# Who issues a kernel's small transfers: two of eight hash-row copies moved from GpSimd to ScalarE, and four of the last turned piece's stores moved from SyncE to GpSimd

## The chip, the cores and the metric

The kernel runs on one core of one Trainium2 chip. The metric is the device time of one execution in microseconds, the median of several runs. Engines are named as the profile names them: PE is TensorE (PEld its weight loads), DVE is VectorE, ACT is ScalarE, POOL is GpSimd, SP is SyncE. SyncE, ScalarE and GpSimd issue the DMA transfers; a "q" behind an engine's name (SPq, ACTq) stands for its sequencer, which does the issuing.

## What is computed

Hash-bucketed attention with 4 batches, 8 heads, 768 positions and a head dimension of 64, followed by a two-layer block with a per-channel PReLU. All arrays are float32 in value (the weights arrive in wider words, which the kernel turns into float32 itself). Cut to what matters:

```python
q_bits = (einsum('bhsd,dk->bhsk', q, proj) > 0)      # 6 hash bits for each row of q and k
k_bits = (einsum('bhsd,dk->bhsk', k, proj) > 0)
mask = q_bucket[:, :, :, None] == k_bucket[:, :, None, :]
scores = where(mask, q @ k.T / sqrt(D), -1e9)
attn = softmax(scores) @ v                           # (B, H, S, D)
x = attn.transpose(0, 2, 1, 3).reshape(3072, 512)
h = x @ w_in                                         # 512 -> 2048
g = maximum(h, 0) + alpha * minimum(h, 0)
out = g @ w_out                                      # 2048 -> 512
```

## The kernel before

**Two stages.** The attention stage works through 16 pairs of heads (`pi`), one after the other. The second stage does the two products of the block for four batches, each product by a seven-product scheme (`ff1`, `ff2`, line 912 issues all their matmuls). Engine instructions are wrapped in `do(...)`, which keeps them in the order in which the program writes them. The DMA issues of the hash rows are not wrapped: a scheduler puts them in their place on the issuing engine.

**One attention pair.** `scores` (L773) makes 12 cells of scores for 128 keys by 384 queries of two heads. Each cell adds two products in one PSUM bank pair: a product of hash bits (`qb`, `kb`, bf16), which is large and negative where the buckets differ, and the product of the scaled `qT` and `kT` (float32). ScalarE turns each cell into exponentials (L784, into `pts`). Cells, turned inputs, hash sums and `totals` share three bank pairs (`two_banks`, L686). `attend` (L806) multiplies with v, and VectorE adds up the exponentials (L792 to L803) so that `totals` (L820) can sum them on TensorE. `divide` (L831) turns the sums on VectorE (L841), takes reciprocals and stores the result (L860).

**The hash rows.** While pair `pi` is in work, `hash_bits(pi + 1)` (L726, called at L1214) makes the next pair's bits. Eight small matmuls (L732) put the hash sums of both halves of q and k in one PSUM bank, and ScalarE's Sign pass (L736) writes them as the bf16 tile `hr`. The bits then have to go to other partitions: eight transfers of 12 rows and 9 KB each (L742), all issued by GpSimd, in the order k, k, q, q of the first half of the columns, then the same of the second half. They write `kb` (one buffer) and `qb` (two). Next on ScalarE is the scaling of the next pair's `qT` (L1215), then the rounding of the next weight piece (`weight_abs`, L599 and L603), the squares of q and k (L714) and another weight piece. On TensorE `attend` and `totals` follow the hash matmuls, and then the next pair's score cells, the first of which reads the first half's bits and the second, third and so on both halves' q bits.

**Weights on the side.** In each pair two raw weight pieces of 512 KB are loaded by GpSimd (`load_weight`, L585; one before the hash rows, one after them), rounded by ScalarE and VectorE, and stored for the second stage by SyncE (L654 and L667, the latter four stores of 448 KB as w_in_s). SyncE also loads q, k and v for later pairs. Early in the second stage GpSimd loads and stores eight pieces of w_out each (L999, L1006).

**Completion semaphores.** In the built program the transfers that GpSimd issues take eight semaphores in turn, and those that SyncE and ScalarE issue take eight others in turn, the two engines together. Each transfer but the first of a semaphore waits, on its issuing engine, for the landing of the transfer that used that semaphore before.

**The end.** Each batch's output pieces are turned in one of two ways. `turn_out` (L1071) turns a finished piece with VectorE (L1076) and stores it with 12 transfers of 32 KB (L1083). In the last block `turn_last` (L1088) turns pieces 5 and 4 of the last batch with TensorE, and ScalarE issues their three stores (L1105, L1114, L1116). `turn_out` runs at the end of each block but the last; for the last batch the pieces that reach it are 2 and 3, piece 3 in the last but one block. The test at L1082 names piece 5 of the last batch, which never comes through `turn_out`, so before the change SyncE issues all the stores there. After its last work each engine reads a flag, branches over a fallback version of the kernel (`general_path`), and waits for what is still open.

Of the kernel before, what the change touches and what calls it, by code (L numbers as in the profile page):

```python
# [407 lines left out]
def fast_path(  # L408
# [12 lines left out]
    nc = tc.nc  # L421
    P = 128
    B, H, S, D = q.shape
# [262 lines left out]
    def two_banks(name):  # L686
        return psum.tile([P, 2, 512], F32, name=name, tag="sc", bufs=3)
# [38 lines left out]
    def hash_bits(pi):  # L726

        ps = two_banks(f"hs{pi}")[:, 0, :CW]
        for half in range(2):
            for n, name in enumerate("kq"):  # L730
                c = D * n + 32 * half
                do(PE.matmul(  # L732
                    ps[c : c + 32], wh2, tr[name, pi][:, half * CW : (half + 1) * CW], start=True, stop=True,
                ))
        raw = pool.tile([P, CW], BF16, name=f"hr{pi}", tag="hr", bufs=1)
        do(ACT.activation(raw, ps, AF.Sign, bias=hb2))  # L736
        bits["q", pi], bits["k", pi] = qbs[pi % 2], kb
        for half in range(2):
            for n, name in enumerate("kq"):
                for s in range(2):  # L740
                    c = D * n + 32 * half + NB * s
                    nc.gpsimd.dma_start(  # L742
                        bits[name, pi][D * s : D * s + 2 * NB, half * CW : (half + 1) * CW], raw[c : c + 2 * NB],
                    )

# [325 lines left out]
    def turn_out():  # L1071
        while to_turn:
            b, p, half, ch = to_turn.pop(0)
            o = late[0].tile([P, CW, 2], F32, name=f"o{b}_{p}", tag="o")
            for i in range(2):
                do(DVE.transpose(o[:, :, i], m2[b, p][:, i]))  # L1076

            src = o.rearrange("p (c w d) i -> p c w (d i)", c=CH, d=32)
            for a in range(DM // 128):
                for c in range(CH):  # L1080
                    cols = slice(half * DM // 2 + 64 * a, half * DM // 2 + 64 * a + 64)
                    queue = nc.gpsimd if (b, p) == (B - 1, 5) and c % 2 else nc.sync  # L1082
                    queue.dma_start(  # L1083
                        out_v[b, ch * CH + c].rearrange("(w r) d -> r w d", r=32)[:, :, cols],
                        src[32 * a : 32 * a + 32, c],
                    )
# [90 lines left out]
    for pi in range(NPAIR):  # L1177
# [35 lines left out]
        if pi + 1 < NPAIR:  # L1213
            hash_bits(pi + 1)  # L1214
            do(ACT.activation(tr["q", pi + 1], tr["q", pi + 1], AF.Copy, scale=DOWN))  # L1215
# [38 lines left out]
    for j, (b, what, n) in enumerate(blocks):  # L1254
# [45 lines left out]
        if j + 1 < len(blocks):  # L1300
            turn_out()
        else:
            turn_last(0)
# [37 lines left out]
```

## Time and profile before

| | us |
|---|---|
| median of 3 runs (lowest, highest) | 880.37 (876.08, 881.94) |
| the profiled execution's own time | 880.52 |
| its span, first to last instruction | 878.6 |
| TensorE busy | 861.8 |
| VectorE busy | 749.9 |
| ScalarE busy | 361.4 |
| GpSimd busy | 130.4 |

The attention stage ends near 316 us, the second stage fills the rest. Times in the views are microseconds from the start of the span unless marked ns. A row of a timeline gives start, length, engine, line, operation, the tile it writes and the tile it reads, and in brackets how long the engine had been idle before it and what ended that. A row of a windows table gives the stretch, its length, then busy time and number of instructions of TensorE, its weight loads, VectorE, ScalarE and GpSimd, and at the end the granted TensorE clock, the busy share of the 16 DMA engines and their GB/s. An entry of the waits view gives total time, number of waits and the longest.

### The profile page before, as it was taken

How to read it: one execution, taken by the hardware profiler on the slowest of the kernel's cores; microseconds unless marked ns; L12 is line 12 of the kernel's file. 1: busy time of each engine (PE TensorE's matmuls, PEld its weight loads, DVE VectorE, ACT ScalarE, POOL GpSimd, SP SyncE). 2: the span in 40 equal slices, each digit the busy share in tenths (PEclk: the TensorE clock that was granted, in tenths of full speed). 3: DMA queues.
4: the chain of work that ended last, by engine and by line, in shares of the span. 5: the costliest groups of instructions: out<-in, count | busy, mean ns of one | idle time of the engine just before them, and what ended most of it. 6: DMA issues, size and time to landing. Idle time of an engine off the chain costs nothing.

```text
span 878.6 us, 14811 instructions
## 1 busy us (share of the span) xinstructions
PE 861.8 (98%) x5458; PEld 577.3 (66%) x5458; DVE 749.9 (85%) x1215; ACT 361.4 (41%) x654; POOL 130.4 (15%) x279
## 2 busy tenths in 40 slices
PE   9999999999998999999999999999999999999996
PEld 4444445444444445559996558996557997557996
DVE  6999989989997987999888769898668988668986
ACT  7776878878676752221112222112222112222111
POOL 1332544424433501120000000000000000000000
PEclk9999999999999999999999999999999999999998
DMA  8865886798696347685433426334435333520242
GB/s 195 174 150 125 196 215 151 166 215 219 166 257 154 116 146 264 209 302 219 147 122 94 167 90 198 112 124 115 141 121 155 142 118 99 176 84 1 96 153 68
DMA packets 171777, 135.36 MB, mean 154 GB/s; under 512 B 126976, under 2 KB 155824, under 8 KB 168112
## 3 DMA queue, kind: packets, MB, share of 16 engines
q1 hardware_dynamic: 158960, 108.44, 43.4%
q0 software_dynamic: 10320, 24.71, 9.3%
q10 hardware_dynamic: 2416, 1.18, 0.5%
q8 instruction: 45, 0.74, 0.3%
q14 instruction: 36, 0.29, 0.1%
HBM read 104.87 MB, written 28.31 MB: 152 GB/s over the span
## 4 chain that ended last, share of the span: by engine, by line
PE 61%; DVE 4%; issue 1%; POOL 0%; ACT 0%; DVEq 0%; ACTq 0%
PE f_0a L912 2%; PE z_4a L912 2%; PE z_7a L912 2%; PE z_3a L912 2%; PE z_6a L912 2%; PE z_5a L912 2%; PE f_4a L912 2%; PE f_3a L912 2%; PE f_2a L912 2%; PE f_1a L912 2%; PE z_2a L912 2%; PE f_5a L912 2%; PE z_1a L912 2%; PE f_7a L912 2%; PE f_6a L912 2%; PE z_2c L912 1%
## 5 line engine op out<-in xcount | busy, mean ns | idle before, releaser
L781 PE MATMUL sc<-qT,kT 64*128 64x384 f32 x768 | 157.4, 487 | 0.0
L784 ACT ACTIVATE pt<-sc 128x768 f32<-128x768 f32 x192 | 152.8, 812 | 8.2 <-PE sc L781 7.9
L814 PE MATMUL av<-pt,vn 128*32 128x385 f32 (+1 forms) x1536 | 127.0, 485 | 0.0
L814 PEld LDWEIGHTS av<-pt,vn 128*32 128x32 f32 x1536 | 50.3, 109 | 73.8 <-issue 71.7
L781 PEld LDWEIGHTS sc<-qT,kT 64*128 64x128 f32 x768 | 70.6, 189 | 41.4 <-issue 40.5
L781 PE MATMUL sc<-qb,kb 64*128 64x384 bf16 x384 | 66.7, 325 | 6.9 <-DMA qb<-hr 5.6
L965 DVE TENSOR_TENSOR g<-g,g 128x384 f32<-128x384 f32 x128 | 68.4, 555 | 2.2
L1029 DVE TENSOR_TENSOR gs<-g,gs 128x768 f32<-128x768 f32 x56 | 53.4, 953 | 1.0
L1029 DVE TENSOR_TENSOR gs<-g 128x768 f32<-128x768 f32 x56 | 53.3, 953 | 0.0
L1021 DVE TENSOR_TENSOR ws<-wl 128x512 f32<-128x512 f32 x56 | 38.5, 688 | 17.3 <-DMA wl<-w_out_s 16.3
L599 ACT ACTIVATE wr<-raw 128x512 int32<-128x512 uint32 x32 | 22.1, 692 | 64.2 <-issue 41.5
L781 PEld LDWEIGHTS <-kb 64*128 64x128 bf16 x384 | 22.0, 94 | 35.5 <-issue 12.3
L792 DVE TENSOR_TENSOR accp<-pt,pt 128x1536 f32<-128x1536 f32 x16 | 28.2, 1760 | 16.6 <-ACT pt L784 16.6
L961 DVE SCALAR_TENSOR_TENSOR g<-h,alpha 128x384 f32<-128x384 f32 x32 | 19.7, 617 | 24.9 <-ACT h L954 24.8
L742 POOL DMA_DIRECT2D kb<-hr x60 | 30.3, 507 | 24.1 <-ACT hr L736 23.5
L742 POOL DMA_DIRECT2D qb<-hr x60 | 29.8, 500 | 8.0 <-issue 4.3
L797 DVE TENSOR_TENSOR accd<-accd,pt 128x1536 f32<-128x1536 f32 x16 | 28.1, 1759 | 2.1 <-ACT kn L714 0.5
L803 DVE TENSOR_TENSOR accd<-accd,accp 128x1536 f32<-128x1536 f32 x16 | 28.1, 1758 | 0.6
L800 DVE TENSOR_TENSOR accp<-accp,pt 128x1536 f32<-128x1536 f32 x16 | 28.1, 1753 | 0.0
L796 DVE TENSOR_TENSOR accd<-pt,pt 128x1536 f32<-128x1536 f32 x16 | 28.0, 1752 | 0.0
L912 PE MATMUL f_0a<-x,wi 128*128 128x384 f32 x64 | 23.5, 489 | 0.0
L912 PE MATMUL f_4a<-x,wi 128*128 128x384 f32 x64 | 23.3, 486 | 0.0
(365 smaller groups left out, 1760.2 us busy)
## 6 DMA issues: line engine op xcount, KB each, us to landing
wi<-w_in_s SPq DMA_DIRECT2D x32, 896.0 KB, 4.7
wl<-w_out_s SPq DMA_DIRECT2D x16, 1024.0 KB, 4.8
wl<-w_out_r SPq DMA_DIRECT2D x12, 1024.0 KB, 4.9
raw<-in_moe_w_in_dram POOLq DMA_DIRECT2D x15, 512.0 KB, 5.2
raw<-in_moe_w_out_dram POOLq DMA_DIRECT2D x14, 512.0 KB, 4.8
w_in_s<-wsi SPq DMA_DIRECT2D x16, 448.0 KB, 6.6
qn<-in_q_dram SPq DMA_DIRECT2D x64, 96.0 KB, 5.2
vn<-in_v_dram SPq DMA_DIRECT2D x16, 384.0 KB, 5.9
```

Of the source, the lines that this page charges most:

```text
L742: nc.gpsimd.dma_start(bits[name, pi][D * s : D * s + 2 * NB, half * CW : (half + 1) * CW], raw[c : c + 2 * NB],)
L781: do(PE.matmul(sc[:, s, :CW], what["k", pi][r, ks], what["q", pi][r, qs], start=first, stop=not first,))
L784: do(ACT.activation(pts[kc][:, g, :, :CW], sc[:, :, :CW], AF.Exp, scale=SCALE / DOWN))
L792: do(DVE.tensor_tensor(accp[pi], p(0), p(1), op=ALU.add))
L797: do(DVE.tensor_tensor(accd[pi], accd[pi], p(5), op=ALU.add))
L800: do(DVE.tensor_tensor(accp[pi], accp[pi], p(2), op=ALU.add))
L803: do(DVE.tensor_tensor(accd[pi], accd[pi], accp[pi], op=ALU.add))
L814: do(PE.matmul(av[pi][D * s + t : D * s + t + 32, g, :w], nat["v", pi][:, s, kc * D + t : kc * D + t + 32], pts[kc][:, g, s, :w], start=(k ...
L912: do(PE.matmul(self.ps[bank], self.left(left, k), self.right(right, k), start=start and k == 0, stop=k == self.nk - 1, skip_group_check=no ...
L965: do(DVE.tensor_tensor(new_g(b, to)[:, i], g_m[b, x][:, i], g_m[b, y][:, i], op=ALU.subtract))
L1021: do(DVE.tensor_tensor(t, w2[b, n, x], w2[b, n, y], op=op))
L1029: do(DVE.tensor_tensor(t, g2[b, n, x], g2[b, n, y], op=ALU.subtract))
```

## The change

In `hash_bits` the two k transfers of the first half go to ScalarE's queue; the other six stay with GpSimd. In `turn_out` the test names piece 3 in place of 5, so that of the 12 stores of the last batch's piece 3 the four with c = 1 go to GpSimd and eight stay with SyncE.

```diff
@@ hash_bits
             for n, name in enumerate("kq"):
                 for s in range(2):
                     c = D * n + 32 * half + NB * s
-                    nc.gpsimd.dma_start(
+                    queue = nc.gpsimd if half or name == "q" else nc.scalar
+                    queue.dma_start(
                         bits[name, pi][D * s : D * s + 2 * NB, half * CW : (half + 1) * CW], raw[c : c + 2 * NB],
                     )
@@ turn_out
                     cols = slice(half * DM // 2 + 64 * a, half * DM // 2 + 64 * a + 64)
-                    queue = nc.gpsimd if (b, p) == (B - 1, 5) and c % 2 else nc.sync
+                    queue = nc.gpsimd if (b, p) == (B - 1, 3) and c % 2 else nc.sync
                     queue.dma_start(
```

One line is added, so that a line number above 742 stands for the line one higher in the changed kernel.

## The prediction

> **What bounds the kernel now.** I read the page first, then the waits of TensorE alone, then windows one attention pair long, then the timelines of the pairs that stand out and of the last 10 us.
>
> ```profile
> PE 861.8 (98%) x5458; PEld 577.3 (66%) x5458; DVE 749.9 (85%) x1215; ACT 361.4 (41%) x654; POOL 130.4 (15%) x279
> ...
> L781 PE MATMUL sc<-qb,kb 64*128 64x384 bf16 x384 | 66.7, 325 | 6.9 <-DMA qb<-hr 5.6
> ```
>
> TensorE is busy 861.8 of 878.6 us, so a change that touches none of its work can win only the 16.8 us that it isn't. The largest named piece of that is 5.6 us in front of the score matmuls, until hash rows have landed.
>
> ```profile
> PE sc L781 <- DMA qb<-hr: 5.6, 3, 3.2
> ```
>
> Only three waits make up the 5.6 us. The windows run from the first hash matmul of one pair (L732) to that of the next; columns: length, then each engine's busy time, granted clock, DMA share.
>
> ```profile
> 97.53:116.51 18.98, 18.98 (x187) 8.91 (x185) 17.98 (x25) 14.91 (x23) 10.35 (x19) 1.00 0.70 168
> 116.51:136.97 20.46, 19.41 (x187) 9.96 (x185) 18.22 (x25) 15.07 (x23) 6.22 (x16) 1.00 0.97 227
> ...
> 174.93:195.68 20.75, 19.30 (x187) 9.85 (x185) 17.89 (x25) 15.08 (x23) 6.03 (x16) 1.00 0.94 223
> 252.62:276.66 24.04, 20.86 (x186) 10.88 (x184) 19.00 (x26) 14.95 (x23) 7.40 (x16) 0.93 0.99 238
> 276.66:296.08 19.42, 19.16 (x186) 9.34 (x184) 18.51 (x25) 14.64 (x23) 10.42 (x18) 1.00 0.41 117
> ```
>
> An undisturbed pair takes 18.98 us, all TensorE. Pairs 6, 9 and 13 (counted by the hash that opens the window) take 1.48, 1.77 and 5.06 us more: 8.31 us, more than the waits, because TensorE is slow after a gap (clock 0.93 in the last; there four matmuls take 1.75 us that take 0.81 before it). These three have the DMA engines 94 to 99% busy, the other windows after the first at most 83%: SyncE is then storing w_in_s. GpSimd in pair 9, in pair 13, and TensorE in pair 13:
>
> ```profile
> 174.37 0.58 POOL L585 DMA_DIRECT2D raw<-in_moe_w_in_dram  x1 [4.80 <-ACT pt L784]
> ...
> 179.78 0.50 POOL L742 DMA_DIRECT2D qb<-hr  x1
> 182.08 0.50 POOL L742 DMA_DIRECT2D qb<-hr  x1 [1.81 <-DMA raw<-in_moe_w_in_dram]
> ```
>
> ```profile
> 257.47 0.50 POOL L742 DMA_DIRECT2D qb<-hr  x1
> 262.31 0.50 POOL L742 DMA_DIRECT2D qb<-hr  x1 [4.34 <-issue]
> ```
>
> ```profile
> 262.62 0.32 PE L781 MATMUL sc<-qb,kb 64*128 64x384 bf16 x1
> 266.13 0.48 PE L781 MATMUL sc<-qb,kb 64*128 64x384 bf16 x1 [3.18 <-DMA qb<-hr]
> 266.13 1.75 PE L781 MATMUL sc<-qT,kT 64*128 64x384 f32 x4
> ```
>
> The eighth row transfer is the late one. The built program says why: GpSimd's transfers take eight completion semaphores in turn, and each waits until the last user of its semaphore has landed. With ten transfers a pair (two raw weight loads, eight rows), the seventh and eighth rows wait for the two raw loads before them. In pairs 6 and 9 the eighth goes out 0.28 us after the raw load lands. In pair 13 that landing (259.10) would have let it go at 259.4, and it goes at 262.31; the profile names nothing for the other 2.9 us. It is the 129th transfer of GpSimd's queue, and follows the landing of the 128th (261.91) by 0.4 us; that this is the cause is a guess.
>
> **Hash rows: what moves.** Each of 15 pairs loses two GpSimd issues (508 ns median each) and gains two ScalarE issues between Sign and the qT scaling. GpSimd then has eight transfers a pair. In the built program every row's semaphore was last used by a row of the pair before, 19 us old, and no row waits for a raw load. The last row is issued sixth, not eighth: about 2.5 us after the first. The orders of TensorE, VectorE and ScalarE (but for the new issues) don't change; on SyncE a v load moves ahead of one q load in most pairs, for data two and three pairs away.
>
> Pair 9: the sixth row goes out near 179.3. Before, rows landed from 183.28 at about 0.17 us each, so it lands near 184.1; it is needed at 185.25. The 1.77 us goes whole. Pair 13: rows landed from 260.06 to 261.58 for the first six and are needed at 261.80 to 262.9, so the hash stall goes. But there VectorE's transpose of the sums (L841) ended only at 263.82, and the third score cell wants its bank at 263.43; pair 14, where it is as late, pays 0.44 for it (window of 19.42). So 5.06 - 0.44 = 4.62. Pair 6: there all rows landed late (the first 126.12, though issued at 118.35; the first cell wanted them at 125.7). The q rows of the first half are now first and second instead of third and fourth: two steps of 0.2 us off a first wait of 0.92, and the 0.13 and much of the slow clock behind it. Bounds 0.4 and 1.48; I take 0.8, nearer the row. Sum: 1.77 + 4.62 + 0.8 = 7.2 us. If the 2.9 us in pair 13 belong to a 129th transfer, that is now the tenth w_out transfer (119 go before them), near 365 us; their last landing is 398.94 and the first load that reads them starts at 407.89, so 8.9 us cover it.
>
> What the two issues cost ScalarE: nearest rows are its own four k loads at the start, with SyncE issuing at the same time, and the idle time that follows in each pair.
>
> ```profile
> 0.75 2.22 ACTq L504 DMA_DIRECT2D kn<-in_k_dram  x4
> ...
> 257.56 0.19 ACT L714 ACTIVATION_READ_ACCUMULATOR kn<-kn 128x1 f32 x1
> 262.55 0.67 ACT L599 ACTIVATE wr<-raw 128x512 int32<-128x512 uint32 x1 [4.80 <-DVE wsi L643]
> ```
>
> 2.22 / 4 = 0.56 us each, so 1.1 us a pair, 17 us over 15 pairs. Behind them on ScalarE stand the qT scaling (ends 254.9, wanted by TensorE at 261.98), a weight pass, two squares, and then the wait for VectorE at L599: 64.2 us of idle time in all, 4.3 us a pair. The 1.1 us lies inside it: nothing on the path. Without that cover it would delay the exps one for one.
>
> Two rules weigh against this. The Trainium skill, *DMA: Bandwidth & Descriptors*, section "Issuing engines are not separate DMA queues", says that spreading DMAs over engines saves only issue time. By it each last row is 2 x 0.5 us earlier and no more: pair 9 keeps 0.46 of its wait of 1.46, pair 13 2.2 of 3.18, a gain of about 3 us. The 1.81 us of idle time ahead of the eighth row, ended by the raw load's landing, is not issue time, so I take 7.2. *Perfetto Trace Analysis*, section "DMA Instruction — HWDGE (DVE, Sync)", says that the descriptor block is locked for one issue at a time. At the start the two engines share it at 0.56 and 0.48 us an issue. In pair 13 SyncE's w_in_s issues take up to 1.83 us each; two such holds are 3.7 us against 4.80 us of cover. Zero by both, with 1.1 us to spare in the second. ScalarE's new transfers also wait for a semaphore last used by a SyncE load; those had landed at least 2 us before Sign ends in all pairs but 13, where it is 0 to 0.6 us.
>
> **Stores at the end.** [...]ScalarE and SyncE share eight semaphores the same way.
>
> ```profile
> 867.97 4.85 SPq L1083 DMA_DIRECT2D out_dram<-o  x5
> ...
> 870.03 0.40 ACTq L1105 DMA_DIRECT2D out_dram<-o  x1
> 871.61 0.36 ACTq L1114 DMA_DIRECT2D out_dram<-o  x1
> 872.10 0.38 ACTq L1116 DMA_DIRECT2D out_dram<-o  x1
> ```
>
> The 12th store went out at 872.50, when ScalarE's store of 870.03 had landed (872.49). SyncE then read the flag, branched (to 876.39) and walked through its final waits to 877.85. Now SyncE has eight stores, none waits so, and it is done near 869; it stands in the final waits at the seventh when the last store lands (875.85), and has 0.9 us of them left: 876.85, a gain of 1.0 us (0 if something else holds the end, 1.5 at most). GpSimd's four issues (0.5 to 0.8 us each by its rows, from 864.7) are done by 868.
>
> **Sum.** 880.52 (profiled, span 878.6) - 7.2 - 1.0 = 872.3 us, 0.9% less. The median shown is 880.37, 0.15 below the profiled run, so no shift. Its runs lie 876.08 to 881.94; stalls of this size varying would do that. For this kernel I take about 1% as what a measurement can tell.
>
> **Rivals.**
> 1. *Only issue time is saved; late rows stay* (saturated DMA engines hold rows whoever issues them). For: pair 6, where all rows were late. Against: pair 9, where seven rows were in by 184.45. Gain 3 + 1 at most, 876.5 to 879.
> 2. *VectorE becomes the bound.* It is 17.9 to 19.0 busy of 18.98, with one more subtraction (0.95) in pairs 12 to 14. For: 0.44 in pair 14. If pair 13 loses a full 0.95 to it, and pair 14 as much again, 872.3 + 1.5 = 873.8.
> 3. *ScalarE is blocked (slower).* Its two issues, or their semaphore waits, hold it longer than the 4.3 us of cover, and the exps come late. It decides from 4.3 + 8.2/15 = 4.9 us a pair, 2.4 us an issue; at 3 us an issue 15 x 1.7 = 26 us are lost, 898. Against: 0.56 us at the start.
> 4. *The end doesn't gain*: 873.3.
>
> **Chances.** The forecast with 2 and 4 as its variants 0.72 (own range 870 to 874.5), rival 1 0.16, rival 3 0.08, more than forecast (pair 6 whole, below 870) 0.04. The 1% line is 871.6, inside the forecast's own range: faster by over 1% 0.35, within 1% 0.57, slower by over 1% 0.08. Range for 8 in 10: 869.5 to 879.
>
> **What would show it.** Right: no wait of L781 for hash rows over 0.9 us, no idle time of GpSimd before a row that a raw load ends, pair 9 at 18.98, pair 13 near 19.4, ScalarE's issues under 0.8 us, the idle time before L599 down by about 1 us a pair, SyncE's last store before 870. Wrong: exps waited for by TensorE, k rows on the ScalarE queue landing after 261 in pair 13, or the 2.9 us still there with GpSimd's sixth row.

## The result and the profile after

The changed kernel takes 873.32 us (median of 11 runs, 871.72 to 874.43), the kernel before in the same group 880.4 us (11 runs, 876.08 to 882.98). The ratio is 0.9918 with a 95% interval of 0.9901 to 0.9935: 0.8% less time. The forecast was 872.3 us. The profiled execution took 873.29 us with a span of 871.5, 7.1 us less than the span of before.

TensorE is busy 859.9 of the 871.5 us (99%). Two groups of the changed kernel's page; line numbers above 742 are one higher than before:

```profile
L782 PE MATMUL sc<-qb,kb 64*128 64x384 bf16 x384 | 64.4, 323 | 1.6 <-DVE st L842 1.3
...
L599 ACT ACTIVATE wr<-raw 128x512 int32<-128x512 uint32 x32 | 22.1, 691 | 37.0 <-DVE wsi L643 19.0
```

The idle time ahead of the score matmuls fell from 6.9 to 1.6 us, and what ended most of it is no longer a hash row. ScalarE's idle time ahead of its weight pass fell from 64.2 to 37.0 us: the two issues are paid there. The waits of TensorE alone:

```profile
PE sm L828 <- DVE accd L804: 1.4, 1, 1.4
PE sc L782 <- DVE st L842: 1.3, 3, 0.6
...
PE z_2c L913 <- DVE m L1051: 0.8, 1, 0.8
PE z_1a L913 <- DVE gs L1030: 0.5, 1, 0.5
```

No wait of TensorE for `qb<-hr` is left in this list; the four lines shown all name VectorE. Two of its weight loads still wait for hash rows in pair 6, 1.1 us in all (1.8 before), and the profiles of e1, e8 and e10 below still have a wait for `qb<-hr` of 0.34 to 0.47 us there. The windows of pairs 9, 13 and 14 (length first, near the end the granted clock and the DMA share):

```profile
173.81:192.79 18.98, 18.98 (x187) 8.88 (x185) 17.88 (x25) 15.19 (x23) 5.03 (x13) 1.00 1.03 242
249.73:269.10 19.37, 19.15 (x186) 9.29 (x184) 18.44 (x25) 14.75 (x23) 8.02 (x14) 1.00 1.09 257
269.10:288.91 19.81, 19.33 (x187) 9.21 (x185) 18.91 (x26) 14.75 (x23) 9.39 (x16) 1.00 0.57 155
```

In pairs 9 and 13 the DMA engines are as full as before (1.03 and 1.09 by the profile's own reckoning, 0.94 and 0.99 before), and the windows are 1.77 and 4.67 us shorter; pair 6 (19.32 us) is 1.14 shorter, pair 14 0.39 longer. The first hash matmul of pair 15 starts at 288.91 us, 7.17 earlier than before. GpSimd in pair 13, where it had been idle for 4.34 us ahead of the eighth row:

```profile
251.52 1.01 POOL L743 DMA_DIRECT2D qb<-hr  x2 [0.96 <-ACT hr L736]
252.53 1.00 POOL L743 DMA_DIRECT2D kb<-hr  x2
253.52 1.00 POOL L743 DMA_DIRECT2D qb<-hr  x2
```

Six rows, one behind the other. ScalarE in the same pair, and all 30 of its row issues (shortest, median and longest in ns; the bracket at L1216 counts the two issues as idle time of ScalarE):

```profile
251.26 1.50 ACTq L743 DMA_DIRECT2D kb<-hr  x2
252.80 0.85 ACT L1216 ACTIVATE qT<-qT 128x768 f32<-128x768 f32 x1 [1.57 <-DMA kb<-hr]
...
259.55 0.68 ACT L599 ACTIVATE wr<-raw 128x512 int32<-128x512 uint32 x1 [3.05 <-DVE wsi L643]
```

```profile
L743 ACTq DMA_DIRECT2D kb<-hr x30: 724/732/1601, 21.1 to 291.2; - x30
```

An issue costs ScalarE 0.73 us in the median, not the 0.56 of the forecast; 3.05 us of the 4.80 us of idle time are left in this pair.

Between pair 15 and TensorE's last matmul 1.2 us are given back (the last matmul ends 6.0 us earlier, not 7.2). VectorE in the first half of that stretch:

```profile
387.63 0.69 DVE L1022 TENSOR_TENSOR ws<-wl 128x512 f32<-128x512 f32 x1 [1.19 <-DMA wl<-w_out_r]
```

It waits 1.19 us for a weight load, and TensorE then waits for `gs` (0.51 us) and `m` (0.78 us; there the kernel before has 0.49). The load's buffer came free late: by the landing records in the trace, 15 of the 16 pieces of the w_out_s store that held it had landed by 379.40 us, the last at 382.13. The profile of the same kernel in another execution (e9 below) has only 0.3 us of this.

From TensorE's last matmul to the end of the span it is 5.91 us, before 7.04.

### The profile page after: what moved, and what is told of

The parts are those of the page before. It is cut to its first block, busy times and chain, and to the rows that moved or that the text cites. A ratio compares the mean times of both kernels' runs of the same rounds, so it can differ in the third digit from the quotient of the medians.

```text
span 871.5 us, 14591 instructions
## 1 busy us (share of the span) xinstructions
PE 859.9 (99%) x5458; PEld 574.1 (66%) x5458; DVE 749.7 (86%) x1215; ACT 363.3 (42%) x654; POOL 119.6 (14%) x253
## 3 DMA queue, kind: packets, MB, share of 16 engines
q10 hardware_dynamic: 3136, 1.46, 0.6%
## 4 chain that ended last, share of the span: by engine, by line
PE 59%; DVE 4%; DMA 2%; issue 1%; POOL 0%; ACT 0%; SPq 0%; DVEq 0%; ACTq 0%; POOLq 0%
PE f_0a L913 2%; PE z_4a L913 2%; PE z_7a L913 2%; PE z_3a L913 2%; PE z_6a L913 2%; PE z_5a L913 2%; PE f_2a L913 2%; PE f_1a L913 2%; PE z_2a L913 2%; PE f_3a L913 2%; PE z_1a L913 2%; PE f_4a L913 2%; PE f_7a L913 2%; PE f_6a L913 2%; PE f_5a L913 2%
## 5 line engine op out<-in xcount | busy, mean ns | idle before, releaser
L782 PE MATMUL sc<-qT,kT 64*128 64x384 f32 x768 | 155.5, 483 | 0.0
L1084 POOL DMA_DIRECT2D out_dram<-o x4 | 2.2, 558 | 474.1 <-DVE o L1077 474.1
L782 PE MATMUL sc<-qb,kb 64*128 64x384 bf16 x384 | 64.4, 323 | 1.6 <-DVE st L842 1.3
L599 ACT ACTIVATE wr<-raw 128x512 int32<-128x512 uint32 x32 | 22.1, 691 | 37.0 <-DVE wsi L643 19.0
L1216 ACT ACTIVATE qT<-qT 128x768 f32<-128x768 f32 x15 | 12.7, 845 | 25.7 <-DMA kb<-hr 19.5
```

Of the source, the lines that this page charges most:

```text
L782: do(PE.matmul(sc[:, s, :CW], what["k", pi][r, ks], what["q", pi][r, qs], start=first, stop=not first,))
```

## The experiments

Each kernel is compared with the kernel before (medians 878.8 to 880.4 us in the groups). The pairs' windows in each profile, in us:

| kernel | median us | ratio to before (95%) | 6 | 9 | 12 | 13 | 14 |
|---|---|---|---|---|---|---|---|
| before | 880.4 | | 20.46 | 20.75 | 18.98 | 24.04 | 19.42 |
| changed | 873.32 | 0.9918 (0.9901 to 0.9935) | 19.32 | 18.98 | 18.98 | 19.37 | 19.81 |
| e1 rows only | 873.97 | 0.9940 (0.9925 to 0.9955) | 19.72 | 18.98 | 18.98 | 19.60 | 19.79 |
| e2 stores only | 879.17 | 1.0000 (0.9983 to 1.0017) | 20.01 | 19.67 | 18.98 | 24.66 | 19.42 |
| e3 one row | 873.79 | 0.9941 (0.9927 to 0.9956) | 20.18 | 18.98 | 18.98 | 19.37 | 19.80 |
| e4 raw load on SyncE | 879.75 | 1.0005 (0.9990 to 1.0020) | 19.45 | 19.21 | 18.98 | 27.61 | 18.98 |
| e5 four rows | 874.15 | 0.9948 (0.9928 to 0.9968) | 19.21 | 19.20 | 18.97 | 19.40 | 19.80 |
| e6 all rows on ScalarE | 906.75 | 1.0330 (1.0302 to 1.0359) | 22.46 | 23.61 | 20.57 | 22.25 | 20.59 |
| e7 sixteen more | 877.27 | 0.9983 (0.9966 to 1.0000) | 20.73 | 19.90 | 20.02 | 20.24 | 19.42 |
| e8 sums on GpSimd | 870.76 | 0.9908 (0.9890 to 0.9926) | 19.75 | 18.98 | 18.98 | 19.49 | 18.98 |
| e9 changed again | 872.47 | 0.9920 (0.9888 to 0.9951) | 18.99 | 18.98 | 18.98 | 19.37 | 19.80 |
| e10 rows and sums | 872.42 | 0.9916 (0.9885 to 0.9947) | 19.84 | 19.35 | 18.98 | 19.24 | 18.98 |
| e11 as e8 | 870.97 | 0.9901 (0.9866 to 0.9936) | 19.65 | 19.09 | 18.98 | 19.25 | 18.98 |
| e12 six stores | 880.12 (one run) | | 19.82 | 20.15 | 18.98 | 25.81 | 19.11 |

**The two parts alone.** Rows only (the first hunk of the change):

> Only the hash rows move (two k rows of each pair to ScalarE); the stores of the last turned piece stay with SyncE. My theory (the eighth row of a pair waits on GpSimd for the landing of a raw weight load that used its completion semaphore before): pairs 9 and 13 lose their stalls (windows 18.98 and about 19.4 us), about 6.0 us less than before of the 7.1 that both parts brought together, 874.3 us if before is 880.4. Rival, only two issues of 0.5 us are saved on GpSimd: about 3 us less, 877.4. Rival, the stores did most of it: under 2 us less.

Stores only (the second hunk):

> Only the four stores move to GpSimd; all eight hash rows stay with GpSimd. My theory: SyncE's twelfth store no longer waits for the landing of ScalarE's first, and the time between TensorE's last matmul and the end of the span goes from 7.04 to about 5.9 us: 1.1 us less than before, 879.3 us if before is 880.4; the windows of pairs 9 and 13 keep their stalls (20.7 and 24.0 us). Rival, the end is held by the landing of ScalarE's last store whatever SyncE does: 0.3 us less or nothing. Rival, the stores and the rows need each other: nothing.

The rows bring 5.4 us of medians (879.4 to 873.97), nearer to the 6.0 expected than to the rival's 3, and pairs 9 and 13 are as forecast. For the stores alone the medians show nothing, but the interval is 0.17% (1.5 us) to either side of one, so that the runs can't tell nothing from the 1.1 us expected. In the profile the stretch from TensorE's last matmul to the end is 7.00 us against 7.04: the expected 5.9 failed there, and the part on e12 below says why.

**Issue time or semaphore: one row instead of two.**

```diff
-                    nc.gpsimd.dma_start(
+                    (nc.scalar if half == 0 and name == "k" and s == 0 else nc.gpsimd).dma_start(
```

> One k row of each pair goes to ScalarE instead of two, stores as before. GpSimd then has nine transfers a pair, and the last of its seven rows takes the semaphore of the first of the two raw loads, issued some 10 us earlier, not that of the second. My theory: the wait goes with the first row moved, so this is as fast as the two-row version, 6 us less than before within 1 us, 874.4 if before is 880.4, pair 9 at 18.98 us. Rival, issue time: the last row is only 0.5 us earlier, so pair 9 keeps about 0.96 us and pair 13 about 2.7 us of its wait; 1.0 to 1.8 us less than before, about 879.

The last four rows on GpSimd in pair 9 of this kernel:

```profile
178.08 1.01 POOL L742 DMA_DIRECT2D kb<-hr  x2
179.08 1.00 POOL L742 DMA_DIRECT2D qb<-hr  x2
```

They go out back to back: the 1.81 us of idle time ahead of the last row are gone, though its issue is only half a microsecond nearer to the first. Pair 9 is at 18.98; by issue time it would have kept about 0.96 us. GpSimd has one transfer fewer per pair, so that the last row's semaphore is that of an older load (in the trace of e3 that load, issued at 164.10, had landed at 169.99). One row moved brings what two bring (873.79 and 873.97 us), but the whole time alone would not decide between the two accounts: with fewer transfers the 129th also leaves pair 13 (see e7).

**The same wait removed with all eight rows left on GpSimd.**

```diff
-        load_weight(i + 3)
+        load_weight(i + 3, nc.sync)
```

> All eight rows stay with GpSimd and so does their issue time; of the two raw weight loads of a pair the one issued just ahead of the rows goes to SyncE. The eighth row then takes the semaphore of the other raw load, issued some 10 us earlier. My theory: GpSimd's eighth row goes out 0.5 us behind the seventh, pair 9 takes 18.98 us and pair 13 about 19.4, and the time is 5 to 6 us less than before (about 875 if before is 880.4), less what SyncE's other transfers lose by the extra load. Rival, issue time: nothing is saved, 880.4 and windows of 20.7 and 24.0 us. Rival, saturated DMA engines hold the rows: the same windows stay long although the rows go out in time.

The last four rows on GpSimd in pair 9, then ScalarE's second weight pass in pair 13 of this kernel:

```profile
178.25 1.03 POOL L742 DMA_DIRECT2D kb<-hr  x2
179.27 1.03 POOL L742 DMA_DIRECT2D qb<-hr  x2
```

```profile
265.80 0.66 ACT L599 ACTIVATE wr<-raw 128x512 int32<-128x512 uint32 x1 [10.48 <-DMA raw<-in_moe_w_out_dram]
```

The mechanism shows in pair 9: no row has moved, yet the eighth follows the seventh at once. In the kernels with the rows and both raw loads unmoved the eighth is issued after 0.62 to 1.81 us of idle time (before, e2, e7 and e12). The window is 19.21 us against 19.67 to 20.75 in those four; the first rival would have kept both the idle time and the window, the second the window. The time as a whole is no better (ratio 1.0005), for a cost that the expectation had named but not sized: in pair 13 SyncE issues the raw load only at 258.05, behind four stores of w_in_s and one of x_s, where GpSimd had issued it at 252.93 in the kernel before. ScalarE's weight pass waits for it until 265.80 us, and the exponentials queue behind that pass. One of the twelve executions took 3240.58 us, for a reason that no trace here shows; the ratio leaves it out.

**How much ScalarE can hide.** Four rows, then all eight:

```diff
-                    nc.gpsimd.dma_start(
+                    (nc.scalar if name == "k" else nc.gpsimd).dma_start(
```

> All four k rows of a pair go to ScalarE, the four q rows stay with GpSimd, stores as before. Theory (ScalarE's idle time of 4.3 us a pair ahead of its weight pass hides the issues, at the 0.73 us each that the changed kernel showed): 4 x 0.73 = 2.9 us a pair are hidden too, so the time is that of rows-only within 1 us, 874 if before is 880, and the idle time of ScalarE ahead of the weight pass goes from 64 us to about 20. Rival, ScalarE's issues hold the exponentials up: each pair loses 1 us or more, 15 us over the kernel, 889.

```diff
-                    nc.gpsimd.dma_start(
+                    nc.scalar.dma_start(
```

> All eight rows of a pair go to ScalarE. 8 x 0.73 = 5.9 us a pair against 4.3 us of idle time. Theory: the cover is gone, ScalarE runs up to 1.6 us late in each pair and TensorE waits for exponentials or free score banks: up to 24 us over 15 pairs on top of what the moved rows win, 880 to 898, and the waits of TensorE name ScalarE or the banks it frees. Rival, ScalarE has more slack than the named idle time: 874 as with four rows.

Four rows cost no more than one or two (874.15 us); the idle time ahead of the weight pass is 13.0 us there (about 20 was expected). With eight the cover is gone. ScalarE in pair 4 of that kernel, and the waits of its TensorE:

```profile
85.83 1.50 ACTq L742 DMA_DIRECT2D kb<-hr  x2
...
91.98 0.84 ACT L1215 ACTIVATE qT<-qT 128x768 f32<-128x768 f32 x1 [6.18 <-DVE wx L615]
```

```profile
PE sc L781 <- ACT pt L784: 15.3, 12, 2.0
PE sc L781 <- DMA qb<-hr: 5.8, 6, 1.7
PE sc L781 <- ACT qT L1215: 3.0, 3, 1.2
```

The eight issues take 6.15 us (85.83 to 91.98), and undisturbed pairs take 20.57 to 20.59 us, 1.60 more than 18.98. The expectation's 5.9 - 4.3 gives the same number, in part by luck: the idle time that the issues use up is only 4.04 us in pair 4 of the kernel before (ahead of L599 at 87.71), so that, taken one for one, 2.1 us would have come out. What hides the other 0.5 us is not shown. The 906.75 us lie above the expected 898 in part because in pairs 6, 9, 11 and 13 the last rows or the scaled `qT` come late as well (the second and third line); pair 2 is long too (23.03 us), and there the eight issues take 6.95 us.

**The 2.9 us that nothing named in pair 13.** The kernel before with sixteen more small transfers:

```diff
+    extra = const.tile([1, 16], F32, name="extra")
+    for j in range(16):
+        nc.gpsimd.dma_start(extra[:, j : j + 1], moe_alpha[j : j + 1].rearrange("(t p) -> t p", p=1))
     load(1, "v")
```

> The kernel before with sixteen additional transfers of four bytes each on GpSimd ahead of its first weight load; they change no semaphore of the transfers behind them (sixteen is twice eight). The 129th transfer of GpSimd is then the second hash row of pair 12, no longer the eighth of pair 13. Theory (GpSimd's queue stops at the 129th transfer until earlier ones have landed): in pair 12 about 2 to 3 us of idle time that nothing names stand ahead of the second row, which was issued 0.5 us behind the first; in pair 13 the eighth row goes out 0.3 us behind the landing of the raw load and that pair is 1.5 to 3 us shorter than 24 us; the whole time is within 3 us of before. Rival, the idle time belongs to pair 13 and its saturated DMA engines: the eighth row there is as late as before, and pair 12 shows nothing.

GpSimd in pair 12 and in pair 13:

```profile
234.67 0.52 POOL L742 DMA_DIRECT2D kb<-hr  x1 [1.83 <-ACT hr L736]
238.13 0.53 POOL L742 DMA_DIRECT2D kb<-hr  x1 [2.94 <-issue]
```

```profile
260.08 0.52 POOL L742 DMA_DIRECT2D qb<-hr  x1 [1.78 <-DMA raw<-in_moe_w_out_dram]
```

The idle time has moved to the 129th transfer, the second row of pair 12, 2.94 us long, in a pair whose DMA engines are not full. Pair 13 is left with the wait for the raw load alone, and takes 20.24 us instead of 24.04. So of the 4.67 us that the change won in pair 13, about 3.8 are the 129th transfer and 0.9 the semaphore. (The halt costs 1.04 us in pair 12 in return; the whole time is 2.2 us less in the medians, within the 3 us expected.)

All twelve kernels here in which GpSimd issues 129 transfers or more halt at that one; in e5 and e6 it issues 105 and 45. With one transfer fewer per pair the 129th is in pair 15 (e3, and 2.82 us in e4):

```profile
291.48 0.51 POOL L742 DMA_DIRECT2D kb<-hr  x1 [0.31 <-ACT hr L736]
294.86 1.00 POOL L742 DMA_DIRECT2D qb<-hr  x2 [2.87 <-issue]
```

In the changed kernel it is the tenth w_out transfer, as the forecast had it:

```profile
356.58 0.76 POOL L1007 DMA_DIRECT2D w_out_s<-wo  x1 [2.02 <-DVE wo L1006]
361.22 0.76 POOL L1007 DMA_DIRECT2D w_out_s<-wo  x1 [3.89 <-DVE f_4p L958]
```

The second of these stores follows the first by 4.64 us; before, the same two are 1.72 us apart (363.87 and 365.59). The difference is 2.92 us. (The VectorE instruction in the bracket only happened to end then: the sums that this store carries were done at 358.0.) The loads behind it start 8.4 us earlier than before, more than the 7.2 us that the pairs had won, so nothing waits. The halt is not a wait for the transfer ahead: here the 128th lands at 364.19 us, 2.97 us after the 129th went out.

**What pairs 13 to 15 still lose, and VectorE's extra subtraction.** The changed kernel, with one edit:

```diff
         if 12 <= pi < 15:
-            sum_x(0, pi - 12, DVE)
+            sum_x(0, pi - 12, POOL)
```

> The changed kernel (both parts), and three subtractions of 0.95 us that VectorE does in pairs 12 to 14 go to GpSimd. Theory (what is left of the losses in pairs 13 to 15, 0.39, 0.83 and 0.3 us, is VectorE with one subtraction more than in other pairs): 1.5 us less than the changed kernel, 871.8 against 873.3, and the waits for VectorE's transposed sums in these pairs are gone. Rival, the subtraction (about 2 us on GpSimd) slows VectorE's own operations or holds up GpSimd's rows: no gain or slower.

```profile
L885 POOL TENSOR_TENSOR x<-x,x x3: 1814/1821/1822, 243.2 to 285.0; 128x768 f32<-128x768 f32 x3
```

A subtraction takes GpSimd 1.82 us, and it has the time. Pair 14 is at 18.98, and a wait of 0.28 us in pair 15 is gone. Pair 13 is not better (19.49; 19.24 and 19.25 in e10 and e11 against 19.37): what it still loses is not this subtraction, or not alone. On one chip, with the stores as the only other difference:

> The changed kernel once more, as the measure for the two others of this group on the same chip. All theories: 873.3 us within 1 us, 0.8% less than before.

> The rows on ScalarE and the three subtractions on GpSimd, but the twelve stores left with SyncE, so that the stores are the only difference to the next kernel. Theory (the moved stores shorten only SyncE's last waits, by 0.3 to 0.8 us in the traces so far): 0.3 to 0.8 us more than the next kernel, 871.4. Rival, the stores give the 1.0 us of the forecast or more: 871.8 or above. Rival, nothing: the same as the next kernel within 0.2 us.

> The changed kernel with the three subtractions on GpSimd, beside the changed kernel itself on one chip. Theory (VectorE's extra subtraction was what pairs 13 to 15 still lost): 1.5 us or more below the changed kernel. Rival, the first measurement of it was a matter of the chip: no difference.

872.47 us for the changed kernel (871.57 to 873.05), 870.97 with the subtractions on GpSimd (869.87 to 872.40): 1.5 us less. (e8, on another chip, has 870.76.) This version has the lowest medians here, 0.9 to 1.0% below the kernel before. Without the moved stores it is 872.42 (870.76 to 874.07): beside the rows, the stores are worth about 1.4 us in these medians, with ranges that overlap; in the profiles the ends differ by 0.95 us (7.54 and 6.59). The 0.3 to 0.8 us expected of them was too little.

**Why the end of e2 is no shorter.**

```diff
-                    queue = nc.gpsimd if (b, p) == (B - 1, 5) and c % 2 else nc.sync
+                    queue = nc.gpsimd if (b, p) == (B - 1, 3) and (c == 1 or c == 0 and a < 2) else nc.sync
```

> As stores-only (all rows on GpSimd), but six stores go to GpSimd instead of four, which moves ScalarE's last store from the first of the eight semaphores that SyncE waits for at the end to the seventh. Theory: SyncE then stands at the seventh of these waits when that store lands, and the end of the span follows the landing by 1.78 us, as in the changed kernel, not by 2.25 as with four stores. Rival, the place among the semaphores doesn't matter: 2.25 us again.

From the landing of ScalarE's last store to the end of the span it is 2.79 us before (875.85 to 878.64), 2.25 in e2 (875.13 to 877.38), 1.77 in e12 (876.56 to 878.33) and 1.78 in the changed kernel (869.72 to 871.50). So the four stores alone do win 0.54 us behind the landing. The profile of e2 hides it, because there that store landed 4.75 us after TensorE's last matmul, against 4.25 before.

The other 0.48 us hang on a place in a row. In e2 ScalarE's last store has the first of the eight semaphores for which SyncE waits in turn, so SyncE stands at the first of its 20 last waits until 875.15 us and has all the others still to do (to 876.43). In the changed kernel it stands at the seventh until 869.74 and is through at 870.55. From TensorE's last matmul to the end it is 5.91, 6.37, 6.59 and 6.69 us in the four profiles that have rows and stores moved (mean 6.39), 6.12 in e12, and 7.04 to 7.61 us in the eight that leave all twelve stores with SyncE (mean 7.32). (e12 is a single execution of each kernel, and its 880.12 us against 880.43 say nothing by themselves.) With 30 row transfers the semaphores of everything behind them shift by 30 places, and that put ScalarE's last store at the seventh.

## Why the prediction was right

- **Pair 9, 1.77 us whole; pair 13, 4.62 us.** 1.77 and 4.67 in the trace. The cause in pair 9, the semaphore of the raw load, is shown twice: one row moved is enough (e3), and no row need move (e4). *DMA: Bandwidth & Descriptors*, section "Issuing engines are not separate DMA queues", of the Trainium skill, says that spreading transfers over engines saves only the time to initiate them. By that pair 9 would have kept 0.46 of its wait of 1.46 us, and none is left. The section leaves out what the issuing engine waits for before it initiates a transfer.
- **How exact the two numbers are is luck.** Pair 9 takes 19.67 to 20.75 us in the four kernels with eight rows and both raw loads on GpSimd (mean 20.12), and 18.98 to 19.35 in the eight with a row or more moved, e6 aside (mean 19.07). Pair 13 takes 24.04 to 25.81 in the three of those four that have their 129th transfer there (mean 24.84), and a mean of 19.39 in the eight. The gains over all profiles are 1.05 and about 5.4 us. They add up to what the forecast had for the two, and not each by itself.
- **The guess of a 129th transfer.** Shown by e7. It was the larger part of pair 13's stall, so over half of the whole gain is a one-time halt of 2.9 us that the change carried from a pair without cover to a place with cover. The forecast had noted that the transfer went out 0.4 us after the 128th had landed; that was chance (in the changed kernel it goes out 2.97 us before). What makes GpSimd halt there no run here shows.
- **Pair 6, 0.8 us.** 1.14 in this pair of profiles. Over all profiles it is 18.99 to 19.84 with two rows or more moved to ScalarE (e6 aside; mean of seven 19.50), and 19.82 to 20.73 in the four with eight rows and both raw loads on GpSimd (mean 20.26): 0.76. That the new order of the rows did it is not shown: e4, with all rows in the old order, has 19.45, and e3, with one row moved, 20.18. Every row's landing there has one piece of 16 that comes late (in the first row of before the 15th piece is in by 124.38 us, the 16th at 126.12), which moving an issue doesn't change.
- **ScalarE's issues, 1.1 us a pair, hidden.** The term was too small (0.73 us each, 1.5 a pair) and the cover was right: nothing on the path at two and at four rows, and 1.60 us a pair at eight. Rival 3's threshold of 4.9 us a pair fits and is not measured: it lies between what four issues take (e5: 3.1 us in most pairs, 4.7 in pair 9) and the 6.15 of eight (e6). Its point, slow issues, was far off. The forecast's margin in pair 13 rests on a wrong reading: it has SyncE's w_in_s issues there at up to 1.83 us, and one took 2.58, so that two of them are 4.41 us and the margin 0.4, not 1.1. It did no harm: in the changed kernel ScalarE's second issue there took 0.74 us beside one of SyncE's of 2.50. The lock on the descriptor block that *Perfetto Trace Analysis*, section "DMA Instruction — HWDGE (DVE, Sync)", describes shows at most in the longest issue, 1.60 us.
- **Stores, 1.0 us.** 1.13 in the profile and 0.93 in the means (7.32 to 6.39). The reason is the one given: SyncE stands at the seventh of its last waits when ScalarE's last store lands, and has 0.8 us of them left (0.9 forecast; 875.85 and 0.9 make 876.75, where the step has 876.85). What the step doesn't say is that the seventh place is owed to the moved rows. With the rows unmoved the same four stores put that one at the first place, and 0.48 us less is won.
- **Rival 2, VectorE.** Half right: pairs 13 to 15 still lose 0.39, 0.83 and 0.28 us, of which 0.44 in pair 14 and 0.34 in pair 15 were there before. Taking three subtractions from VectorE ended the losses of pairs 14 and 15, not that of pair 13, and brought 1.5 us in the medians.
- **Not foreseen:** 1.2 us given back at the start of the second stage in the profiled execution. e12, where the rows haven't moved, has gaps of 0.44 and 0.78 us in front of the same two products, where the changed kernel has 0.51 and 0.78, so it needs no moved rows; it differs from execution to execution (before 0.49 us and e8 0.48, in front of the second alone).

The sum of the trace: 7.17 in the pairs, 1.2 given back, 1.13 at the end: 7.1 us, as the spans and the medians have it.

## What to carry to other kernels

When one transfer in a row of equal ones goes out late, ask which semaphore it waits for and whose landing that is: count the transfers of the queue modulo the number of its completion semaphores, because one transfer fewer, or another large load elsewhere, may do more than another engine. Moving an issue to a second engine is free only up to the idle time behind it there, which the row of the next waiting instruction gives (4.3 us a pair in the mean here: four issues are free, eight cost 1.6 us in an undisturbed pair), and a load moved behind a queue of large stores pays for them. A gain that a part shows together with another may not be its own: run the parts alone, and read the profile where the runs are too coarse for the part.

## What the runs showed of the hardware

- GpSimd's queue halts for 2.8 to 2.9 us at its 129th transfer: 2.94 us in e7, 2.92 in the changed kernel, 2.9 before, 2.87 in e3, 2.82 in e4. It follows the count of transfers, whatever their size (sixteen of four bytes moved it by sixteen), and not the landing of the 128th. The most that a kernel here issues is 181 (e7), so whether it comes again is not shown.
- Of the 16 pieces of a transfer one lands up to 2.7 us behind the others, at places that differ between executions (126.12 behind 124.38 before, 382.13 behind 379.40 after). TensorE's wait in pair 6 and the 1.2 us given back follow such a piece; why it is late no run here shows.
- The same transfer of 12 rows takes GpSimd 0.51 us to issue and ScalarE 0.73, in the median (60 and 30 issues of the changed kernel; the longest of ScalarE's 1.60).
